# Loading the second unit's rows and gates in the tile program, right behind the plan of units

## The chip, the cores and the metric

One Trainium2 chip, one core of it. The metric is the device time of one launch in microseconds (us). The five engines are PE (TensorE), ACT (ScalarE), DVE (VectorE), POOL (GpSimd) and SP (SyncE, which here only issues transfers). PEld is TensorE's weight load, and a name with q (SPq, DVEq) is the engine's own sequencer at a register, wait, branch or DMA-issuing instruction.

## What is computed

Pooled attention, then a mixture of experts on its output, all in fp32:

```
k_p, v_p = mean of k, v over groups of 8 along the sequence (576 -> 72)
attn     = softmax(q @ k_p.T / 8) @ v_p          # 8 batches x 8 heads, head size 64
x        = attn as [4608, 512]
e        = argmax(x @ w_gate)                    # one of 8 experts for each row
out[row] = gate[row] * (relu(x[row] @ w1[e]) @ w2[e])   # 512 -> 1024 -> 512
```

## The kernel before

**Two programs in one launch.** The first is a tile program (`attention`, then `plan`): waits between its instructions are put in for it from the tiles and DRAM tensors that they read and write, and the order on each engine is the order in which the code is written. It runs the attention in 36 tiles of 128 rows, picks each row's expert, and scatters the row with its gate and its token number to the DRAM tensor `dispatched` (`xs` in the code), where every expert has a region. `plan` (lines 651 to 707, on VectorE) then cuts the regions into units of at most 512 rows and writes the table `tab`, one line for each unit: how many halves of 128 rows it has (column K_U), where its four blocks of 128 rows begin (K_ROW), whether the expert changes. Lines 704 to 706 write the last columns.

The second is the expert program (`experts`, from line 710): five programs written out by hand, one for each engine, with semaphores of its own. It stands in one critical section of the tile program. SP enters that section for all (line 727): it waits there for what is outstanding, and the other engines wait for SP (under line 1521).

**A unit in the expert program.** SP loads the unit's rows (`xload`, line 1225): four blocks of 256 KB into the buffer XE[u % 2], line 1249, and four gates of 1 KB (gate and token of 128 rows) into GT, line 1238. PE transposes the rows (`xt`, line 806, matmuls on line 812), ACT and DVE write them as a high and a low part (lines 1030 and 1045), PE multiplies by w1 (`mm1`, line 859, eight pieces f of 24 matmuls), ACT and DVE form the hidden layer (lines 967 and 988), PE multiplies by w2 (line 881), DVE scales by the gate (line 1170), POOL scatters to the output (line 1349).

**Around the change.** Unit 0 (the first 512 rows of expert 0) is begun in the tile program already: its rows and gates are loaded at lines 435 and 436, its transposes stand at line 452, and six of its eight pieces of the first product run on line 462 under and behind `plan`. `last_hidden` (line 643) is the last of that. SP's last work in the tile program are two transfers of empty rows behind the regions of experts 0 and 1 (line 636, with their places from line 635).

In the expert program PE runs the last two pieces of unit 0's first product (line 859), then transposes blocks 0 and 1 of unit 1 (`xt01(1)`), multiplies the first 12 matmuls of unit 0's last block by w2, transposes blocks 2 and 3 of unit 1 (`xt23(1)`) and goes on with w2. The third group of transposes waits until DVE has written the low part of block 0, the fourth until it has written that of block 1. SP marks unit 0's loads as landed (lines 1313 to 1316), issues `xload(1)` with line numbers read from `tab` by value loads (line 740), and then the eight weight loads of expert 1 (line 1321). POOL's six transfers of empty rows behind the other regions (line 1344) wait for unit 1's loads; SP's `xload(2)` waits for those six.

Of the kernel before, what the change touches and what calls it, by code (L numbers as in the profile page):

```python
# [10 lines left out]
F32 = mybir.dt.float32  # L11
# [7 lines left out]
P = 128  # L19
B, H, S, D = 8, 8, 576, 64  # L20
N, DM, NE, FF = 4608, 512, 8, 1024
# [14 lines left out]
CAP = N + P  # L36
# [11 lines left out]
K_U, K_SW, K_ROW, K_ST, K_AH, NK = 0, 1, 2, 6, 7, 8  # L48
# [30 lines left out]
def attention(ctx, outer, tc, q, k, v, wg, w1v, w2v, xs, W, cst, carry, tab, banks):  # L79
    nc = tc.nc  # L80
# [5 lines left out]
    early, u0 = ExitStack(), {"XE": cst["keep"].tile([P, 4, DM], F32, name="XE0"), "GT": cst["keep"].tile([P, NU, 4, 2], F32, name="GT")}  # L86
# [356 lines left out]
    def x_open():  # L443
        early.close()
        m1 = outer.enter_context(tc.tile_pool(name="m1", bufs=1, side="right", reuse_waits="tile"))
        u0["H"] = m1.tile([P, 2, 8, 512], F32R, name="H")
        u0["X"] = m1.tile([P, 2, 4, 512], F32R, name="X")

    def x_split(s):
        bank, o = (pm, pq)[s % 2], slice(s * P, (s + 1) * P)  # L450
# [194 lines left out]
            hidden(f)  # L645
            multiply(12)

    return u0, more_hidden, last_hidden


def plan(tc, sb, carry, cst, tab, between, after):
# [59 lines left out]
def experts(ctx, tc, xs, w1v, w2v, out, tab, W, ident, empty, scr, u0, banks):  # L711
    nc = tc.nc
    sb = ctx.enter_context(tc.tile_pool(name="m2", bufs=1))
    ST = sb.tile([P, 8, 1024], F32, name="ST")
    XE, GT = (u0["XE"], sb.tile([P, 4, DM], F32, name="XE1")), u0["GT"]
    X, H = u0["X"], u0["H"]
    XH, XL, HH, HL = X[:, 0], X[:, 1], H[:, 0], H[:, 1]
    Y2 = sb.tile([64, 512], F32, name="Y2")
# [6 lines left out]
    pe, act, dve, sp, pool = nc.tensor, nc.scalar, nc.vector, nc.sync, nc.gpsimd  # L725

    with tc.tile_critical():
        names = ("P_xt", "P_h", "P_y", "A_x", "A_h", "A_s1", "A_s2", "V_x", "V_h", "V_y", "V_s1", "V_s2", "V_1", "G_y", "G_s1", "G_s2")
        Q = {n: tc.alloc_semaphore(n) for n in names}
        sx = [[tc.alloc_semaphore(f"sx{i}{s}") for s in range(4)] for i in range(2)]  # L730
        st = [tc.alloc_semaphore(f"st{i}") for i in range(2)]
# [6 lines left out]
        def entry(eng, a, u, lo, hi):  # L738
            r = regs.get((eng, a, u))
            return eng.value_load(tab[u : u + 1, a : a + 1], min_val=lo, max_val=hi) if r is None else r  # L740
# [389 lines left out]
        def ahead(eng, yes, no):  # L1130

            with eng.If(u0[eng] == 1):
                yes()
            with eng.Else():
                no()
# [19 lines left out]
        def dve_unit(u):  # L1155
# [45 lines left out]

            dve.wait_ge(st[u % 2], 64 * (u // 2 + 1))
            dve.reciprocal(out=GT[:, u, :, 0], in_=GT[:, u, :, 0])
            n = entry(dve, K_U, u, 1, 8)
            if u > 0:
                hidden_lo(u)
# [18 lines left out]
        def xload(u):  # L1225


            if u == 2:
                sp.wait_ge(se, 16 * (NE - 2))
            if u >= 2:  # L1230
                sp.wait_ge(Q["P_xt"], 4 * (u - 1))

            rows_of = []

            def gates():

                for s in range(4):
                    sp.dma_start(out=GT[:, u, s, :], in_=xs[ds(rows_of[s], P), DM:]).then_inc(st[u % 2], 16)

            def block(s, apart, rows=True):  # L1240
                r = rows_of[s]
                to, sem = XE[u % 2][:, s, :], sx[u % 2][s]
                if rows and apart:
                    for j in range(4):
                        o = slice(32 * j, 32 * j + 32)
                        sp.dma_start(out=to[o].rearrange("p (g d) -> p g d", g=4),
                                     in_=xs[ds(r, P), j * P : (j + 1) * P].rearrange("(g t) d -> t g d", g=4)).then_inc(sem, 16)
                elif rows:
                    sp.dma_start(out=to, in_=xs[ds(r, P), 0:DM]).then_inc(sem, 16)
                    sp.sem_inc(sem, 48)  # L1250
                else:
                    sp.sem_inc(sem, 64)

            rows_of.extend(entry(sp, K_ROW + s, u, 0, NE * CAP - P) for s in range(4))
            n = entry(sp, K_U, u, 1, 8)

            def blocks(apart):
                for s in range(2):
                    block(s, apart)
                with sp.If(n > 4):  # L1260
                    block(2, apart)
                    with sp.If(n > 6):
                        block(3, apart)
                    with sp.Else():
                        block(3, apart, False)
                with sp.Else():
                    for s in range(2, 4):
                        block(s, apart, False)

            if u < 2:  # L1270
                blocks(False)
                return gates()
            with sp.If(entry(sp, K_U, u - 1, 1, 8) > 2):
                blocks(True)
            with sp.Else():
                blocks(False)
            gates()
# [33 lines left out]
        def sp_start():  # L1311
            def yes():
                sp.sem_inc(Q["P_h"], AF_PE)
                sp.sem_inc(Q["P_xt"], 4)
                for s in (*sx[0], st[0]):
                    sp.sem_inc(s, 64)

            ahead(sp, yes, lambda: xload(0))
            xload(1)
            for i in range(8):  # L1320
                sp.dma_start(out=ST[:, i, :].rearrange("p (c f) -> p c f", c=4 if i < 4 else 2), in_=load_piece(w1v, w2v, 1, i)).then_inc(sg[i], 16)
            count(sp)
# [202 lines left out]
```

## Time and profile before

| what | us |
|---|---|
| median of 3 runs | 635.15 (633.09 to 635.31) |
| the profiled execution | 631.38 |
| its span, first to last instruction | 629.6 |
| TensorE busy | 602.3 (96%) |
| VectorE / ScalarE / GpSimd busy | 354.4 / 240.2 / 240.7 |

The profiled execution is 3.77 us under the median, and 1.78 us of it lie outside the span. All times of rows are microseconds from the start of the span; durations are microseconds or, where a row gives min/median/max, nanoseconds. In a row of the timeline the last bracket is the idle time of that engine ahead of the instruction and what ended it.

### The profile page before, as it was taken

What the parts mean: (1) busy time and instruction counts of PE and PEld (TensorE: products, weight loads), DVE (VectorE), ACT (ScalarE), POOL (GpSimd) and SP (SyncE); (2) the same over time, 40 slices, a digit from 0 to 9 for tenths busy, and PEclk for the clock granted to TensorE, in tenths of its full rate; (3) what the DMA queues carried; (4) which work ended last, traced back from release to release, by engine and by line L of the source; (5) the groups of instructions that cost most, each with busy time, mean ns of one, the idle gap of its engine ahead of it and who ended that gap; (6) DMA issues with size and microseconds to landing.
All of it is one profiled execution on the core that took longest, in us unless ns stands there. A gap on an engine that the chain in (4) does not pass through costs nothing.

```text
span 629.6 us, 13468 instructions
## 1 busy us (share of the span) xinstructions
PE 602.3 (96%) x4412; PEld 513.0 (81%) x4412; DVE 354.4 (56%) x731; ACT 240.2 (38%) x453; POOL 240.7 (38%) x289
## 2 busy tenths in 40 slices
PE   6989999999997999999999999999998999999995
PEld 6778978888876888889898889888897888888994
DVE  7698887889762124467777433854156664133220
ACT  2577666886512014065354311523034641011110
POOL 7457656744421121468445311251107660101101
PEclk9999999999999999999999999999999899999999
DMA  9999996992324930619667551075105453100001
GB/s 326 363 267 258 300 311 209 254 265 70 125 111 135 300 107 2 216 41 297 221 173 267 153 170 36 3 210 167 40 33 164 132 147 71 55 0 36 36 4 53
DMA packets 93937, 96.47 MB, mean 153 GB/s; under 512 B 43102, under 2 KB 74846, under 8 KB 93792
## 3 DMA queue, kind: packets, MB, share of 16 engines
q1 hardware_dynamic: 85808, 74.27, 41.0%
q0 software_dynamic: 7440, 20.50, 8.8%
q8 instruction: 60, 0.98, 0.6%
q14 instruction: 85, 0.70, 0.4%
q10 hardware_dynamic: 544, 0.02, 0.0%
HBM read 72.68 MB, written 26.00 MB: 157 GB/s over the span
## 4 chain that ended last, share of the span: by engine, by line
PE 76%; DVE 6%; issue 5%; DMA 3%; POOL 3%; ACT 3%; SPq 2%; DVEq 0%; ACTq 0%; POOLq 0%
PE pU L881 33%; PE pP L859 20%; PE pq L859 10%; PE pU L299 4%; DMA XE<-in_v_dram 2%; PE pP L283 2%; PE pP L462 2%; POOL dispatched L406 2%; PE pS L263 2%; PE pq L253 1%; SPq L228 1%; ACT W L1057 1%; PE pm L207 1%; DVE mx L267 1%; PE pq L462 1%
## 5 line engine op out<-in xcount | busy, mean ns | idle before, releaser
L881 PE MATMUL pU<-W,H 128*128 128x512 f32 x912 | 216.2, 397 | 0.0
L881 PEld LDWEIGHTS pU<-W,H 128*128 128x128 f32 x912 | 171.3, 188 | 41.0
L859 PE MATMUL pP<-X,W 128*128 128x512 f32 (+3 forms) x748 | 144.0, 347 | 3.7 <-DVEq L1398 1.5
L859 PEld LDWEIGHTS pP<-X,W 128*128 128x128 f32 x748 | 123.6, 189 | 20.4 <-DVEq L1398 2.0
L1349 POOL DMA_INDIRECT out_dram<-Y,GT x51 | 53.0, 1039 | 193.3 <-DVE Y L1170 167.4
L1065 POOL TENSOR_TENSOR W<-ST,W 128x1024 fp32r<-128x1024 f32 x30 | 77.4, 2591 | 89.9 <-ACT W L1057 89.4
L967 ACT ACTIVATE H<-pP 128x512 fp32r<-128x512 f32 (+1 forms) x67 | 35.9, 536 | 196.7 <-PE pP L859 158.1
L1170 DVE TENSOR_SCALAR Y<-pU,GT 128x512 f32<-128x512 f32 x36 | 26.9, 749 | 110.5 <-PE pU L881 109.0
L988 DVE SCALAR_TENSOR_TENSOR H<-pP,H 128x512 fp32r<-128x512 f32 (+2 forms) x73 | 42.1, 579 | 71.5 <-ACT H L967 69.0
L859 PE MATMUL pq<-X,W 128*128 128x512 f32 (+3 forms) x364 | 73.7, 351 | 1.1 <-DVE H L988 0.6
L859 PEld LDWEIGHTS pq<-X,W 128*128 128x128 f32 x364 | 60.8, 191 | 10.1 <-DVE H L988 1.1
L1057 ACT CAST W<-ST 128x1024 fp32r<-128x1024 f32 x56 | 57.1, 1054 | 2.9 <-DMA ST<-in_moe_w_dram 2.9
L299 PE MATMUL pU<-V,pt 110*128 110x146 f32 (+3 forms) x468 | 56.7, 283 | 1.4 <-ACT pt L284 0.8
L299 PEld LDWEIGHTS pU<-V,pt 110*128 110x128 f32 (+3 forms) x468 | 51.4, 179 | 3.1 <-ACT pt L284 1.8
L1065 DVE TENSOR_TENSOR W<-ST,W 128x1024 fp32r<-128x1024 f32 x26 | 46.8, 1801 | 3.5 <-ACT W L1057 2.5
L967 ACT ACTIVATE H<-pq 128x512 fp32r<-128x512 f32 (+1 forms) x33 | 17.8, 541 | 79.5 <-PE pq L859 55.1
L406 POOL DMA_INDIRECT dispatched<-xe,ix x36 | 38.0, 1054 | 15.6 <-POOL ix L368 7.0
L988 DVE SCALAR_TENSOR_TENSOR H<-pq,H 128x512 fp32r<-128x512 f32 (+2 forms) x35 | 20.8, 595 | 28.2 <-ACT H L967 20.3
L284 ACT COPY pt<-pP 110x384 f32<-110x384 f32 x72 | 30.8, 479 | 6.1 <-PE pP L283 4.9
L276 ACT ACTIVATE P<-sd 128x576 f32<-128x576 f32 x36 | 24.8, 689 | 19.3 <-DVE sd L270 16.2
L172 POOL TENSOR_TENSOR raw<-raw 128x768 f32<-128x768 f32 (+1 forms) x18 | 27.0, 1498 | 12.1 <-DMA raw<-in_v_dram 11.4
L267 DVE TENSOR_REDUCE mx<-pS 128x8 f32<-128x576 f32 x36 | 27.1, 752 | 6.8 <-PE pS L263 4.4
(186 smaller groups left out, 621.8 us busy)
## 6 DMA issues: line engine op xcount, KB each, us to landing
ST<-in_moe_w_dram SPq DMA_DIRECT2D x56, 512.0 KB, 4.6
raw<-in_k_dram SPq DMA_DIRECT2D x12, 768.0 KB
raw<-in_v_dram SPq DMA_DIRECT2D x11, 768.0 KB
XE<-dispatched SPq DMA_DIRECT2D x104, 64.0 KB, 2.0
qa<-in_q_dram SPq DMA_DIRECT2D x24, 256.0 KB
w<-in_moe_w_dram SPq DMA_DIRECT2D x8, 512.0 KB
XE<-dispatched SPq DMA_DIRECT2D x15, 256.0 KB, 3.8
qa<-in_q_dram SPq DMA_DIRECT2D x2, 1024.0 KB
```

Of the source, the lines that this page charges most:

```text
L172: return lambda: eng.tensor_tensor(out=out, in0=raw[:, :, 0:n], in1=raw[:, :, n : 2 * n], op=ALU.add)
L267: nc.vector.tensor_reduce(out=mx, in_=s4, axis=AX.X, op=ALU.max)
L284: take(out=pt[t][a][0:R], in_=pPs[a][0:R, 0 : 3 * P])
L299: nc.tensor.matmul(pu[p0 : p0 + n, a, h * VW : (h + m) * VW], lhsT=pt[t][a][0:r, c % 3 * P + p0 : c % 3 * P + p0 + n], rhs=Vs[g % 2][0:r, ...
L406: apart(nc.gpsimd.indirect_dma_start(out=xs, out_offset=bass.IndirectOffsetOnAxis(ap=at, axis=0), in_=rows, in_offset=None))
L859: r = pe.matmul(out=pH[g % 3][:, :m], lhsT=w1s(w, f, k), rhs=x, start=i == 0, stop=i == len(passes) - 1)
L881: r = pe.matmul(out=pY[:, s % 2, :], lhsT=h, rhs=w[:, k * 512 : (k + 1) * 512], start=start and i == 0, stop=stop and i == len(ps) - 1, sk ...
L967: act.activation(out=HH[:, f, o], in_=src[:, o], func=AF.Relu).then_inc(Q["A_h"], 1)
L988: return dve.scalar_tensor_tensor(out=dst[:, f, to], in0=src[:, at], scalar=0.0, in1=f32(HH[:, f, at]), op0=ALU.max, op1=ALU.subtract)
L1057: act.copy(out=(W1H if i < 4 else W2H)[:, o], in_=ST[:, i, :]).then_inc(Q["A_s1" if i < 4 else "A_s2"], 1)
L1065: eng.tensor_tensor(out=(W1L if i < 4 else W2L)[:, o], in0=ST[:, i, :], in1=f32((W1H if i < 4 else W2H)[:, o]), op=ALU.subtract).then_inc( ...
L1349: pool.indirect_dma_start(out=out, out_offset=bass.IndirectOffsetOnAxis(ap=GT[:, u, s, 1:2].bitcast(I32), axis=0), in_=Y[:, s, :], in_offs ...
```

## The change

The buffer XE1, which holds the rows of odd units, moves from the expert program's pool to the pool that the attention opens for unit 0 (`x_open`). A new function `second_load` reads the four places of unit 1's blocks from the second line of `tab` and issues unit 1's four blocks and four gates on SP; it is called behind `plan`, ahead of `last_hidden`. In the expert program SP's `xload(1)` goes, and SP marks those loads as landed at once. All four blocks are loaded whatever the unit's size; the old code left out blocks that the unit does not have. Two smaller edits: DVE drains behind the reciprocal of a unit's gates (line 1203, 13 times in this execution), and from unit 2 on SP waits ahead of a unit's gates until DVE has written the first hidden piece of the unit two before.

```diff
--- before.py
+++ after.py
@@ -445,6 +445,7 @@
         m1 = outer.enter_context(tc.tile_pool(name="m1", bufs=1, side="right", reuse_waits="tile"))
         u0["H"] = m1.tile([P, 2, 8, 512], F32R, name="H")
         u0["X"] = m1.tile([P, 2, 4, 512], F32R, name="X")
+        u0["XE1"] = m1.tile([P, 4, DM], F32, name="XE1")
 
     def x_split(s):
         bank, o = (pm, pq)[s % 2], slice(s * P, (s + 1) * P)
@@ -645,7 +646,20 @@
             hidden(f)
             multiply(12)
 
-    return u0, more_hidden, last_hidden
+    def second_load():
+        rows = [nc.sync.value_load(tab[1:2, K_ROW + s : K_ROW + s + 1], min_val=0, max_val=NE * CAP - P) for s in range(2)]
+        for s in range(4):
+            if s == 2:
+                rows += [nc.sync.value_load(tab[1:2, K_ROW + s : K_ROW + s + 1], min_val=0, max_val=NE * CAP - P) for s in range(2, 4)]
+            nc.sync.dma_start(out=u0["XE1"][:, s, :], in_=xs[ds(rows[s], P), 0:DM])
+        for s in range(4):
+            nc.sync.dma_start(out=u0["GT"][:, 1, s, :], in_=xs[ds(rows[s], P), DM:])
+
+    def at_last():
+        second_load()
+        last_hidden()
+
+    return u0, more_hidden, at_last
 
 
 def plan(tc, sb, carry, cst, tab, between, after):
@@ -712,7 +726,7 @@
     nc = tc.nc
     sb = ctx.enter_context(tc.tile_pool(name="m2", bufs=1))
     ST = sb.tile([P, 8, 1024], F32, name="ST")
-    XE, GT = (u0["XE"], sb.tile([P, 4, DM], F32, name="XE1")), u0["GT"]
+    XE, GT = (u0["XE"], u0["XE1"]), u0["GT"]
     X, H = u0["X"], u0["H"]
     XH, XL, HH, HL = X[:, 0], X[:, 1], H[:, 0], H[:, 1]
     Y2 = sb.tile([64, 512], F32, name="Y2")
@@ -1201,6 +1215,7 @@
 
             dve.wait_ge(st[u % 2], 64 * (u // 2 + 1))
             dve.reciprocal(out=GT[:, u, :, 0], in_=GT[:, u, :, 0])
+            dve.drain()
             n = entry(dve, K_U, u, 1, 8)
             if u > 0:
                 hidden_lo(u)
@@ -1234,6 +1249,8 @@
 
             def gates():
 
+                if u >= 2:
+                    sp.wait_ge(Q["V_h"], 8 * (u - 2) + 1)
                 for s in range(4):
                     sp.dma_start(out=GT[:, u, s, :], in_=xs[ds(rows_of[s], P), DM:]).then_inc(st[u % 2], 16)
 
@@ -1267,7 +1284,7 @@
                     for s in range(2, 4):
                         block(s, apart, False)
 
-            if u < 2:
+            if u == 0:
                 blocks(False)
                 return gates()
             with sp.If(entry(sp, K_U, u - 1, 1, 8) > 2):
@@ -1316,7 +1333,8 @@
                     sp.sem_inc(s, 64)
 
             ahead(sp, yes, lambda: xload(0))
-            xload(1)
+            for s in (*sx[1], st[1]):
+                sp.sem_inc(s, 64)
             for i in range(8):
                 sp.dma_start(out=ST[:, i, :].rearrange("p (c f) -> p c f", c=4 if i < 4 else 2), in_=load_piece(w1v, w2v, 1, i)).then_inc(sg[i], 16)
             count(sp)
```

## Rows read from the trace of the kernel before

**Rows 1.** The page's first two parts: busy time of PE with its share of the span, and in 40 equal slices the tenths of full speed that TensorE's clock was granted.

```profile
PE 602.3 (96%) x4412; PEld 513.0 (81%) x4412; DVE 354.4 (56%) x731; ACT 240.2 (38%) x453; POOL 240.7 (38%) x289
...
PEclk9999999999999999999999999999999899999999
```

**Rows 2.** The view of waits for PE from 200 us to the end, its first line: who waited for whom, us in total, times, the longest.

```profile
PE pP L859 <- DVE H L988: 1.4, 2, 1.1
```

**Rows 3.** The timeline of PE from 184 to 206 us: start, length, line, tiles, count, idle time before and what ended it.

```profile
186.22 2.96 PE L462 MATMUL pq<-X,W 128*128 128x512 f32 x12
190.71 5.88 PE L859 MATMUL pP<-X,W 128*128 128x512 f32 x24 [1.53 <-DVEq L1398]
197.46 0.75 PE L812 MATMUL pS<-ident,XE 128*128 128x128 f32 x4 [0.86 <-DMA XE<-dispatched]
199.48 0.75 PE L812 MATMUL pS<-ident,XE 128*128 128x128 f32 x4 [1.28 <-DMA XE<-dispatched]
199.98 3.05 PE L881 MATMUL pU<-W,H 128*128 128x512 f32 x12
202.87 1.11 PE L812 MATMUL pS<-ident,XE 128*128 128x128 f32 x8
203.74 2.59 PE L881 MATMUL pU<-W,H 128*128 128x512 f32 x10
```

**Rows 4.** The view of waits of SP's own queue, whole span.

```profile
SPq L435 <- DMA dispatched<-xe,ix: 19.3, 3, 12.6
...
SPq L727 <- PE pq L462: 4.2, 1, 4.2
...
SPq L727 <- DMA dispatched<-empty: 3.5, 2, 2.8
```

**Rows 5.** The last instruction of line 727 on SP between 180 and 190 us, behind which the other engines are let in: count, ns min/median/max, first and last start in us.

```profile
L727 SPq NOP  x1: 18/18/18, 189.3 to 189.3; - x1
```

**Rows 6.** The timeline of all engines around the end of the plan: the last write of the table, and SP's two transfers of empty rows.

```profile
178.61 1.49 SPq L636 DMA_DIRECT2D dispatched<-empty  x2
...
181.82 0.22 DVE L706 TENSOR_SCALAR tab<-off,R 128x4 int32<-128x4 f32 x1
```

**Rows 7.** Two stretches of the view by stretches, behind those two transfers and up to PE's last tile-program matmul: length, busy time of PE, PEld, DVE, ACT, POOL, granted clock, share of the DMA engines, GB/s.

```profile
182.05:183.70 1.65, 1.65 (x9) 1.33 (x8) 0.58 (x1) 0.08 (x1) 0.00 (x0) 1.00 0.04 6
183.70:189.20 5.50, 5.48 (x24) 4.09 (x22) 0.69 (x1) 0.52 (x1) 0.00 (x0) 1.00 0.00 0
```

**Rows 8.** The chain that ended last, in order of time, where it runs over SP: one value load (three pieces, the next begins at 192.00), and the first two blocks of unit 1.

```profile
191.39 0.28 SPq L740
...
192.00 0.26 SPq L740
...
194.36 0.37 SPq L1249
...
194.99 4.45 DMA XE<-dispatched
```

**Rows 9.** The instructions of line 1238 on SP between 190 and 203 us, and those of line 1343 on POOL, which come right behind POOL's wait for unit 1's gates.

```profile
L1238 SPq DMA_DIRECT2D GT<-dispatched x4: 333/333/1089, 197.1 to 199.4; - x4
...
L1343 POOLq TENSOR_LOAD <-tab x6: 288/296/318, 202.2 to 208.1; - x6
```

**Rows 10.** The page's list of DMA issues: count, KB each, median us from issue to landing.

```profile
XE<-dispatched SPq DMA_DIRECT2D x104, 64.0 KB, 2.0
```

**Rows 11.** The timelines of SP and POOL around unit 0's loads in the tile program: the last gate, and the next scatter to the same tensor, which waits for it.

```profile
158.12 0.43 SPq L436 DMA_DIRECT2D GT<-dispatched  x1
...
163.72 1.02 POOL L406 DMA_INDIRECT dispatched<-xe,ix  x1 [5.85 <-DMA GT<-dispatched]
```

**Rows 12.** The timeline of DVE from 197 to 202 us.

```profile
199.35 0.18 DVE L1203 RECIPROCAL GT<-GT 128x4 f32<-128x4 f32 x1 [1.34 <-issue]
199.47 0.69 DVE L1045 TENSOR_TENSOR X<-pS,X 128x512 fp32r<-128x512 f32 x1
200.88 0.69 DVE L1045 TENSOR_TENSOR X<-pS,X 128x512 fp32r<-128x512 f32 x1 [0.72 <-ACT X L1030]
```

**Rows 13.** The view by stretches again (columns as in group 7): the pause between the programs, a stretch with little work for PE, and the one stretch of the expert program in which the granted clock was half.

```profile
189.18:190.71 1.53, 0.00 (x1) 0.00 (x0) 0.00 (x0) 0.00 (x0) 0.00 (x0) 1.00 0.00 0
...
484.58:487.52 2.94, 1.22 (x8) 1.00 (x8) 2.29 (x6) 1.33 (x3) 2.17 (x3) 1.00 0.88 295
...
488.12:491.53 3.41, 3.41 (x19) 3.41 (x18) 1.11 (x4) 2.29 (x4) 3.05 (x3) 0.50 0.87 270
```

**Rows 14.** The chain that ended last at a small unit's end: a drain that is there already, and the one reciprocal of gates on the chain behind 200 us.

```profile
286.19 0.03 DVEq L1165
286.22 0.05 issue
...
288.47 0.16 DVE GT L1203
```

**Rows 15.** Timelines of DVE, ACT and SP: the first hidden piece of unit 1, the first use of expert 1's weights, and the rows of units 2 and 3.

```profile
223.00 5.35 SPq L1246 DMA_DIRECT2D XE<-dispatched  x8
...
227.15 0.69 DVE L988 SCALAR_TENSOR_TENSOR H<-pq,H 128x512 fp32r<-128x512 f32 x1 [2.57 <-issue]
...
247.54 2.02 ACT L1057 CAST W<-ST 128x1024 fp32r<-128x1024 f32 x2
...
263.04 1.65 SPq L1249 DMA_DIRECT2D XE<-dispatched  x3
```

## The prediction, made before the changed kernel was run

> **What bounds the kernel now.** I read the page first: PE is busy for 602.3 of the 629.6 us of the span [rows 1], so a change can give or take only what PE stands still for, or the clock it runs at. The waits of PE say where it stands still: behind 200 us the largest entry is 1.4 us over two waits [rows 2], so nothing that the change touches late in the run has much to give. The place of the change is the passage from the tile program to the expert program, and there the timeline of PE shows three holes [rows 3]. PE's last tile-program matmuls end at 186.22 + 2.96 = 189.18. Then 1.53 us pass until line 859 begins at 190.71; that is the entry of the critical section. After those 24 matmuls PE waits 0.86 us for block 0 of unit 1 and, four transposes later, 1.28 us for block 1. These last two, 2.14 us together, are what the change aims at.
>
> What opens the entry is in SP's own waits [rows 4]: line 727 waited 3.5 us for the two transfers of empty rows to land, and last, for 4.2 us, for PE's matmuls. So the entry asks for every transfer that is under way as well as for the engines, and only because the transfers were long done did PE end it; SP passed it at 189.3 [rows 5], 0.1 us behind PE. The same list shows that a tile-program load from `dispatched` waits for the writes to it to land (line 435, 12.6 us at the longest).
>
> **The change part by part.**
>
> *Removed: PE's waits for unit 1's rows.* First the bound from PE alone. Eight transposes without a wait take 203.74 - 202.87 = 0.87 us until w2 begins [rows 3]. Behind line 859, which ends at 196.59, w2 would then begin near 197.3 instead of 199.98, 2.7 us earlier. But DVE is next. The fourth group of transposes waits for the low part of block 1, and DVE cannot begin block 0's before its reciprocal at 199.35, ahead of which it was reading its registers and waited for nobody [rows 12]. With the transposes early, the two low parts follow one another: 199.47 + 0.1 for the new drain + 2 x 0.69 = 200.95. PE arrives there at 197.3 + 2.8 for 12 matmuls = 200.1 and waits some 0.9 us; four transposes of 0.12 later w2 goes on at 201.45 instead of 203.74. **Gain 2.3 us**, between 2.1 (the two waits alone) and 2.7.
>
> *Added: eight transfers that the entry has to wait for.* The table is complete at 181.82 + 0.22 = 182.04 [rows 6]. Two value loads at 0.6 us (192.00 - 191.39) [rows 8] end at 183.2, hidden behind the empty rows: their transfers begin at 178.61 and 180.1 [rows 6], SP's 3.5 us of waiting for them from 180.1 on end at 183.7 [rows 4], and the DMA engines fall to a share of 0.04 behind 182.05 and to 0.00 behind 183.70 [rows 7]. Block 0 can so be issued at 183.9. Block 1 follows 0.63 us later (194.99 - 194.36) [rows 8], and is done issuing at 185.15; the two other value loads take it to 186.35, blocks 2 and 3 to 187.6. The four gates began between 197.1 and 199.4, where the first took 1.09 us and the others 0.33 [rows 9], so a pace of 0.53 to 0.77: the last gate is issued at 189.2 to 189.9. Its landing is not shown by itself. From below, the page has 2.0 us for the landing of 64 KB [rows 10]; POOL, which waited for these very loads, read its table at 202.2, 2.8 us behind the last issue [rows 9]; and the last gate of unit 0 was issued at 158.12 while the scatter that waited for it began at 163.72, 5.6 us later [rows 11]. I take 2.2, since the DMA engines are idle in this stretch [rows 7], as they were not beside unit 0. So the last gate lands at 191.4 and SP passes the entry at some 191.6 instead of 189.3. **Cost 2.3 us.** The ends: issues at 0.43 us each [rows 11] and a landing of 2.0 give 183.7 + 1.2 + 7 x 0.43 + 2.0 = 189.9, a delay of 0.7; the slow issue and 5.6 give 195.5, a delay of 6.2.
>
> *What the longer pause does to TensorE's clock.* PE has no work between 189.18 and the entry, so its pause grows from 1.53 to 3.8 us. After 1.53 us the granted clock stayed at 1.00, which is 2.4 GHz [rows 13]. After a stretch of 2.94 us in which PE was busy for 1.22, it was 0.50 (1.2 GHz) from 488.12 for 3.41 us [rows 13]. A pause of 3.8 us without any matmul is more idleness than either row has, and the second is the nearer. In 3.41 us at half speed PE does half its work: **cost 1.7 us**; the ends are 0 and twice that. The Trainium skill (TensorE: Matmul & The Clock Gate, Part 1: The HAM clock gate) makes the slow clock the default that only activity lifts. By that rule the fall is due, and the sum is 1.8; by the row of the 1.53 us pause alone it would be 0.1.
>
> *Moved earlier, at no cost.* Without `xload(1)` SP comes to the weights of expert 1 some 6 us earlier and POOL to its six transfers some 7 us earlier. Both go on overlapping each other; ACT first casts those weights at 247.54 [rows 15], and the rows of unit 2, which wait for POOL's six, were issued at 223.00 and are wanted late in unit 1. There is nothing behind them that PE waits for. XE1 in its new place lies over buffers whose readers were through long before 183 us. If that cover failed, one more wait of the size of 1.3 us would stand at the passage.
>
> *The drains.* The present drain of line 1165 holds DVE for 0.03 us and 0.05 of idling [rows 14]. The chain shows one reciprocal of gates on it behind 200 us, at 288.47 [rows 14]. **Cost 0.1 us**; if all 13 were on it, 1.1.
>
> *The wait ahead of the gates.* SP's loads of unit 3 were issued from 263.04 on, while the first hidden piece of unit 1, for which they will wait, was being written at 227.15 [rows 15]. Behind SP's wait stand only the stagings of the next weights, which wait for later steps of the same units. Cost nothing; with the cover gone, a gate would be late at line 1170, and the bound is one landing of 2 us.
>
> **The sum.** -2.3 + 2.3 + 1.7 + 0.1 = +1.8 us. The profiled execution would go from 631.38 to 633.2. It lies 3.77 us under the median of the runs shown, so I put the difference on the median: 635.15 + 1.8 = 636.95, said as 637.0. A measurement of this kernel can tell about 0.5% from no change, 3.2 us; the forecast is no change that can be told.
>
> **The rivals.**
>
> *The clock holds* (0.18). The loads land as forecast, PE's pause falls so that the clock stays at 2.4 GHz as it did after 1.53 us. Sum +0.1: 635.3. Against it speaks the row at 488.12.
>
> *Slower: the last gate lands late* (0.17). Unit 0's gates took up to 5.6 us to their reader. With that in place of 2.2 the entry is opened 3.4 us later still: 635.15 + 1.8 + 3.4 = 640.4, and the longer pause makes the clock's fall surer. It decides from the point where the entry is more than 3.7 us late (3.7 - 2.3 + 1.7 + 0.1 = 3.2), a last gate landing behind 192.9. For it: eight issues and four value loads in one queue, the gates at its end. Against it: nothing else moves at that time.
>
> *The loads are free* (0.07). The entry does not wait for them, or they land before PE's last matmul. Then only the gain and the drain are left: 635.15 - 2.2 = 632.95, still within 0.5%. The Trainium skill (DMA: Bandwidth & Descriptors, Rules for kernel authors) advises just this, to issue early, compute, and wait late. Against it: line 727 did wait for transfers [rows 4], and 189.9 is the earliest landing that the rows allow.
>
> *Not what it says, or something elsewhere* (0.06). The loads are held behind a wait that the tile program adds and I do not see, or the stretch of half clock at 488.12 comes or goes with the new phase: 1.7 us either way around 635.3, with a tail to both sides.
>
> **How the numbers follow.** The forecast has 0.52. Its own bounds (landing 2.0 to 2.8, gain 2.1 to 2.7, clock 0 to 3.4) make about 634.5 to 639. The range takes in the clock rival and the lower half of the late gate, and at the bottom almost the free loads: 633.0 to 640.0. Left out are the later half of the late gate (0.09), most of the free loads (0.05) and tails (0.04). Slower by over 0.5%, that is above 638.3: 0.17, nearly all from the late gate and the upper end of the clock. Faster by over 0.5%, under 631.97: 0.04, from the tails alone, for even free loads do not reach it. Within: 0.79.
>
> **What the changed profile would show.** Right: line 812's waits for XE gone from PE's list; in SP's waits line 727 last released by transfers from `dispatched`, not by PE; a pause of PE of 3 to 5 us ahead of line 859, and behind it a stretch of granted clock 0.50; w2's second stretch no earlier than now; POOL's transfers of line 1344 some 5 us earlier. Wrong: line 859 beginning near 190.7 would mean that the entry does not wait, or that the loads are faster than every row here; a pause of 3.8 us with the clock at 1.00 would take the clock term out; a gain at the passage that is lost again behind 250 us would mean that I overlooked a late consumer.

## The result: slower by 0.5 to 0.75%, and the profile after

| | before | after | ratio, 95% interval |
|---|---|---|---|
| first measurement, medians of 6 runs each | 635.09 us | 639.83 us | 1.0075 [1.0054, 1.0096] |
| second, on another chip, medians of 35 and 12 runs | 635.68 us | 638.54 us | 1.0048 [1.0029, 1.0067] |
| profiled execution | 631.38 us, span 629.6 | 638.89 us, span 637.2 | |

The change costs 4.7 us by the first measurement and 2.9 by the second. The forecast was +1.8: the sign holds, the range (633.0 to 640.0) holds by 0.2 us, the size does not. Chips differ by some 5 us on the kernel before (medians of 634.65, 630.98 and 635.68 on the three of the experiments), so everything below goes by ratios against before on the same chip.

The page after, its first two parts, as in [rows 1]:

```profile
PE 604.9 (95%) x4412; PEld 515.3 (81%) x4412; DVE 355.3 (56%) x731; ACT 240.3 (38%) x453; POOL 241.4 (38%) x289
...
PEclk9999999999998899999999999999999899999999
```

PE is busy 2.6 us longer with the same 4412 matmuls, and the clock has two new dips near 200 us. So a part of the loss is clock and the rest is waiting. The timeline of PE at the passage, columns as in [rows 3]:

```profile
187.70 2.96 PE L463 MATMUL pq<-X,W 128*128 128x512 f32 x12
194.04 7.41 PE L873 MATMUL pP<-X,W 128*128 128x512 f32 x24 [3.38 <-DVEq L1416]
201.29 1.11 PE L826 MATMUL pS<-ident,XE 128*128 128x128 f32 x8
202.16 3.05 PE L895 MATMUL pU<-W,H 128*128 128x512 f32 x12
206.88 1.33 PE L826 MATMUL pS<-ident,XE 128*128 128x128 f32 x8 [1.67 <-DVE X L1059]
```

Read it against [rows 3] from the end of the tile program, which the profiled execution reaches at 190.66 instead of 189.18: 1.48 us were lost before that, the distance hardly changes from 56 us on, and the change touches nothing there. The pause grew from 1.53 to 3.38 us (+1.85). The 24 matmuls take 7.41 instead of 5.88 us (+1.53). The two waits for `XE` are gone: eight transposes in one row. But a new wait of 1.67 us for DVE stands at the third group, so that from the end of the 24 matmuls to that group 5.43 us pass instead of 6.28. Of the gain of 2.3 only 0.85 arrived.

The stretches of the clock, columns as in [rows 7]; the third is the time in which ACT and DVE read their registers:

```profile
194.40:197.81 3.41, 3.41 (x10) 2.64 (x9) 1.29 (x2) 1.08 (x2) 2.68 (x3) 0.50 0.36 96
...
208.05:211.46 3.41, 3.41 (x10) 2.69 (x9) 1.36 (x3) 0.85 (x3) 0.00 (x0) 0.50 1.01 277
...
201.50:205.00 3.50, 3.50 (x20) 2.82 (x18) 0.75 (x2) 0.59 (x1) 1.27 (x3) 1.00 1.03 372
```

Two stretches of 3.41 us at a granted clock of 0.50 (1.2 GHz): the first behind the pause of 3.38, the second behind the new wait of 1.67. At half speed the second costs 3.41 / 2 = 1.7.

SP's waits, and line 741's last instruction (the old 727), as in [rows 4, 5]:

```profile
SPq L741 <- DMA GT<-dispatched: 1.2, 2, 1.0
```

```profile
L741 SPq NOP  x2: 13/16/18, 192.6 to 636.0; - x2
```

The first of these two stands at the entry, which is now opened by the gates' landing: SP passes it at 192.6, 1.9 us behind PE's end. The chain that ended last, in order of time, says how SP came there:

```profile
181.57 3.81 DMA dispatched<-empty
185.52 0.37 SPq L654
...
186.50 0.27 SPq L653
...
188.88 0.33 SPq L656
...
190.46 1.71 DMA GT<-dispatched
```

The empty rows have landed at 185.38, the blocks go out from 185.52 with the value loads of line 653 between them, the last gate at 190.46, and it lands 1.71 us later.

What came earlier, by the timelines of SP and POOL (start, length, line, tiles, count):

```profile
195.07 9.26 SPq L1339 DMA_DIRECT2D ST<-in_moe_w_dram  x8
...
196.38 0.60 POOL L1362 DMA_DIRECT2D dispatched<-empty  x1 [0.17 <-issue]
```

Before, they began at 199.81 (6.71 us for the eight) and 203.53. They now run beside the value loads with which ACT and DVE read unit 1's sizes. Those, after (count, ns min/median/max, first and last start):

```profile
L754 ACTq TENSOR_LOAD <-tab x2: 984/1006/1029, 202.6 to 203.8; - x2
L794 ACTq TENSOR_LOAD <-tab x1: 813/813/813, 201.5 to 201.5; - x1
L754 DVEq TENSOR_LOAD <-tab x2: 449/763/1077, 203.5 to 204.9; - x2
L794 DVEq TENSOR_LOAD <-tab x1: 881/881/881, 202.3 to 202.3; - x1
```

and the same before:

```profile
L740 ACTq TENSOR_LOAD <-tab x2: 274/276/277, 197.2 to 197.7; - x2
L780 ACTq TENSOR_LOAD <-tab x1: 277/277/277, 196.6 to 196.6; - x1
L740 DVEq TENSOR_LOAD <-tab x2: 306/306/306, 198.1 to 198.7; - x2
L780 DVEq TENSOR_LOAD <-tab x1: 317/317/317, 197.5 to 197.5; - x1
```

Three reads on ACT took 0.83 us and now 2.8; three on DVE 0.93 and now 2.4. Ahead of its reciprocal, and of the low part that PE waits for, DVE now idles 2.82 us, where it was 1.34 [rows 12].

Last, the small units. PE, after, with the holes of interest in brackets:

```profile
279.46 1.22 PE L873 MATMUL pq<-X,W 128*128 128x256 f32 x8 [1.22 <-DVE H L1002]
...
296.24 3.97 PE L873 MATMUL pP<-X,W 128*128 128x384 f32 x21 [1.13 <-issue]
```

Before, they were 0.61 and 0.30; the distance between the kernels grows by 0.68 and 0.45 there. The ledger of the profiled executions is thus 1.85 + 1.53 - 0.85 + 1.7 + 1.1 = 5.3 us for the change, plus 1.5 from ahead of the passage, against 7.5 between their times; 0.7 I did not place. Against the medians' 4.7 and 2.9, the ledger without the second stretch of half clock is 3.6.

The profiles are one execution each, but the mean granted clock is on record for every execution: 0.9916 on average over the 12 of the second measurement, 0.9940 over the 35 of before beside them. An estimate from these is that the clock took (0.9940 - 0.9916) x 637 = 1.5 of the 2.9 us, if PE had work throughout, and waiting the other 1.4.

### The profile page after: what moved, and what is told of

Read it like the earlier page. It is cut to its first block, busy times and chain, and to the rows that moved or that the text cites. A ratio compares the mean times of both kernels' runs of the same rounds, so it can differ in the third digit from the quotient of the medians.

```text
span 637.2 us, 13480 instructions
## 1 busy us (share of the span) xinstructions
PE 604.9 (95%) x4412; PEld 515.3 (81%) x4412; DVE 355.3 (56%) x731; ACT 240.3 (38%) x453; POOL 241.4 (38%) x289
## 4 chain that ended last, share of the span: by engine, by line
PE 71%; DVE 9%; issue 8%; DMA 4%; POOL 3%; ACT 3%; SPq 1%; DVEq 1%; ACTq 0%; POOLq 0%
PE pU L895 30%; PE pP L873 21%; PE pq L873 10%; PE pU L299 3%; DMA XE<-in_v_dram 2%; PE pP L283 1%; DMA raw<-in_v_dram 1%; DVE mx L267 1%; PE pS L263 1%; PE pq L253 1%; DVE xe L315 1%; POOL raw L172 1%; POOL dispatched L406 1%; ACT W L1071 1%; DVE sd L270 1%
## 5 line engine op out<-in xcount | busy, mean ns | idle before, releaser
L873 PE MATMUL pP<-X,W 128*128 128x512 f32 (+3 forms) x748 | 145.6, 349 | 6.6 <-DVEq L1416 3.4
L873 PEld LDWEIGHTS pP<-X,W 128*128 128x128 f32 x748 | 124.9, 191 | 23.5 <-DVEq L1416 3.8
L1002 DVE SCALAR_TENSOR_TENSOR H<-pP,H 128x512 fp32r<-128x512 f32 (+2 forms) x73 | 42.0, 579 | 70.8 <-ACT H L981 69.1
L1002 DVE SCALAR_TENSOR_TENSOR H<-pq,H 128x512 fp32r<-128x512 f32 (+2 forms) x35 | 20.8, 594 | 27.9 <-ACT H L981 24.0
```

Source lines behind the costliest of these rows:

```text
L873: r = pe.matmul(out=pH[g % 3][:, :m], lhsT=w1s(w, f, k), rhs=x, start=i == 0, stop=i == len(passes) - 1)
L1002: return dve.scalar_tensor_tensor(out=dst[:, f, to], in0=src[:, at], scalar=0.0, in1=f32(HH[:, f, at]), op0=ALU.max, op1=ALU.subtract)
```

## The experiments

Three groups, each on one chip with its own runs of before: e1 to e4, e5 to e8, e9 to e12. The theory: the entry waits for the gates, the pause lowers the clock, and the streams moved earlier spoil the gain. The rivals: the drain, the added loads alone, and the issuing pace of SP.

**e1_added: the transfers alone.** Before, with the loads also made in the tile program into tiles that nobody reads; the old `xload(1)` stays.

```diff
+        u0["XE1"] = m1.tile([P, 4, DM], F32, name="XE1")
+        u0["GT1"] = cst["keep"].tile([P, 4, 2], F32, name="GT1")
...
+            nc.sync.dma_start(out=u0["GT1"][:, s, :], in_=xs[ds(rows[s], P), DM:])
...
-    return u0, more_hidden, last_hidden
+    return u0, more_hidden, at_last
```

> The kernel before, with the eight transfers of second_load added in the tile program into buffers that nobody reads; the old loads of unit 1 stay where they were, so nothing is gained and nothing moves earlier. It prices the entry alone. Theory (the entry waits for the last gate, and the longer pause lowers the clock): PE's pause ahead of line 859 is 3.2 to 3.8 us instead of 1.53, behind it 3.4 us at half clock, and the time is 3.4 us (0.5%) over before; PE still waits for XE. Rival (the entry costs little, the loss of the changed kernel is elsewhere, in the drains and in what was moved): under 1 us over before.

Ratio 1.003 [1.0012, 1.0048], +1.9 us, where I had expected 3.4. PE and the stretch of half clock:

```profile
194.71 5.87 PE L874 MATMUL pP<-X,W 128*128 128x512 f32 x24 [3.29 <-DVEq L1413]
201.63 0.75 PE L827 MATMUL pS<-ident,XE 128*128 128x128 f32 x4 [1.05 <-DMA XE<-dispatched]
```

```profile
203.16:206.58 3.42, 2.93 (x9) 2.54 (x10) 1.51 (x3) 0.58 (x1) 0.00 (x0) 0.50 0.60 145
```

The entry term is shown by itself: +1.76 of pause, and slower in time, with nothing moved and nothing gained. The clock fell only 8.4 us behind the pause's end (0.4 in the change), after the waits for `XE`, and the 24 matmuls ran at full speed; why so late stays open.

**e2_warm: work in the pause.** After, with eight more matmuls that nobody reads behind the last hidden piece.

```diff
+        for _ in range(8):
+            nc.tensor.matmul(pm, lhsT=w1s(W[:, 0], 0, 0), rhs=u0["X"][:, 0, 0, :], start=True, stop=True, skip_group_check=True)
```

> The changed kernel, with eight extra matmuls of 128x512 into a bank that nobody reads behind the tile program's last ones; PE so works until about the landing of the last gate and the pause in which it has nothing to do is some 1.5 us again. Theory (clock): the first half-clock stretch goes and line 859 (now 873) takes 5.9 us instead of 7.4; the time falls by 1.5 us against the changed kernel, to about 1.005 of before; if the fall at 208 us came from the first fall, that goes too, and it is 3 us. Rival (the pause costs by its length alone): no change against the changed kernel, 1.0075, or more by what the extra matmuls add.

Ratio 1.0107 [1.0085, 1.0128]. PE:

```profile
195.09 7.42 PE L875 MATMUL pP<-X,W 128*128 128x512 f32 x24 [2.29 <-DVEq L1418]
207.00 1.95 PE L828 MATMUL pS<-ident,XE 128*128 128x128 f32 x8 [4.49 <-issue]
```

The expectation failed: 2.29 us of pause were left and the clock fell all the same. The 4.49 us of waiting for nothing that the profile shows make the time unfit to judge the clock. One packet of instructions (0.02 MB) was moved between 203 and 206 us; whether PE waited for it is not shown. Inconclusive.

**e3_late_both: the two streams held back.** After, with SP's weights and POOL's six transfers of empty rows waiting until DVE has written unit 1's first two low parts.

```diff
+            sp.wait_ge(Q["V_x"], 6)
             for i in range(8):
                 sp.dma_start(out=ST[:, i, :]...
...
+            pool.wait_ge(Q["V_x"], 6)
             for e in range(2, NE):
```

> The changed kernel, with SP's eight weight loads of expert 1 and POOL's six transfers of empty rows held until DVE has written the low part of block 1 of unit 1 (V_x at 6); these are the two streams that the change moved earlier. Theory (DVE's and ACT's value loads took 0.45 to 1.08 us instead of 0.31 and 0.28 because these streams ran beside them): value loads at 0.28 to 0.31 again, PE's wait ahead of the third group of transposes 0.9 us instead of 1.67 or less, no second half-clock stretch; the time falls by 1 us from the wait alone and by 2.5 us with the clock, to about 1.004 of before. Rival (the value loads are slow for another reason, such as code being loaded at that time): value loads stay at about 1 us and the time at 1.0075.

Ratio 1.0031 [1.0011, 1.0052]. PE, and the value loads:

```profile
195.06 7.43 PE L873 MATMUL pP<-X,W 128*128 128x512 f32 x24 [3.39 <-DVEq L1418]
...
206.43 1.31 PE L826 MATMUL pS<-ident,XE 128*128 128x128 f32 x8 [0.18 <-DVE X L1059]
```

```profile
L754 ACTq TENSOR_LOAD <-tab x2: 277/278/280, 203.1 to 203.6; - x2
L754 DVEq TENSOR_LOAD <-tab x2: 304/304/305, 204.0 to 204.6; - x2
```

The reads are back at 0.28 and 0.30 us, PE's wait at 0.18. From the end of the 24 matmuls (202.49) to the third group 3.94 us pass, 6.28 - 3.94 = 2.34 less than before: the forecast's gain, at its size. Pause and half clock stay, and no second stretch of half clock follows. The time by itself does not tell e3 from the change (1.0048 [1.0029, 1.0067] in e9); the trace does, and so do e11 and e12 below.

**e4_nodrain: the drain.** After without it.

```diff
             dve.reciprocal(out=GT[:, u, :, 0], in_=GT[:, u, :, 0])
-            dve.drain()
```

> The changed kernel without the drain behind the reciprocal of the gates. Theory (a drain holds DVE's sequencer, which then passes its branches and register reads only behind the reciprocal, at each small unit): the first reduction of the small unit near 275 us begins 0.3 us behind the reciprocal instead of 0.96, the waits of PE at 278 and 295 us fall from 1.2 and 1.1 to about 0.6 and 0.4 us, and the time falls by 1 to 1.5 us, to about 1.0055 of before. Rival (a drain costs 0.1 us, and the later holes come from the shifted clock): the time stays within 0.3 us.

Ratio 1.0038 [1.0016, 1.0061]. The two holes at the small units are back at 0.60 and 0.45 us, the passage is as in after (pause 3.09, wait 1.73). So the drain makes the holes and not the passage. No second stretch of half clock follows the wait of 1.73, so such a wait does not by itself bring one. The twelve times spread from 633.76 to 641.89 us, and the ratio cannot be told from that of the change.

**e5_late_weights and e6_late_pool: one stream held.** The edit of e3, its first line alone and its second alone.

```diff
+            sp.wait_ge(Q["V_x"], 6)
             for i in range(8):
```

```diff
+            pool.wait_ge(Q["V_x"], 6)
             for e in range(2, NE):
```

> The changed kernel with only SP's eight weight loads held until DVE has written the low part of block 1 of unit 1; POOL's six transfers stay early. Theory (the weights, 4 MB written into SBUF, slow the value loads): value loads of ACT and DVE near 202 us at 0.28 and 0.31 us, the wait of PE there under 0.3 us, the time as with both held, about 1.003 of before. Rival (POOL's transfers slow them): value loads near 0.8 to 1.1 us and the wait 1.7 us, the time at 1.0075.

> The changed kernel with only POOL's six transfers of empty rows held until DVE has written the low part of block 1 of unit 1; the weight loads stay early. Theory (the weights slow the value loads): value loads near 0.8 to 1.1 us and a wait of PE of about 1.7 us as in the changed kernel, the time near 1.0075. Rival (POOL's transfers): value loads at 0.28 and 0.31 us, the wait under 0.3 us, about 1.003.

Ratios 1.0006 [0.9987, 1.0024] and 1.0011 [0.9997, 1.0025]. I had taken the weights alone to be the culprit, or else POOL's six alone. Neither is: each edit by itself brings the wait down, to 0.39 and 0.18 us. But the two are not alike. Three of e5's reads still take 0.52 to 0.56 us, none of e6's does. The reads of e5, then one row of e6 (the rows with x3 and x4 hold later reads too):

```profile
L794 ACTq TENSOR_LOAD <-tab x1: 532/532/532, 198.5 to 198.5; - x1
L754 ACTq TENSOR_LOAD <-tab x4: 275/280/555, 199.2 to 204.8; - x4
L754 DVEq TENSOR_LOAD <-tab x3: 303/306/519, 199.9 to 206.9; - x3
```

```profile
L754 ACTq TENSOR_LOAD <-tab x4: 274/280/289, 199.6 to 205.2; - x4
```

How full the transfer engines are at the reads, by the same view by stretches as above, e5 first, then e6:

```profile
198.50:201.30 2.80, 2.80 (x17) 2.40 (x16) 0.75 (x2) 1.18 (x3) 1.27 (x3) 1.00 0.56 213
```

```profile
199.10:201.50 2.40, 2.40 (x16) 2.08 (x15) 0.75 (x2) 1.30 (x3) 0.00 (x0) 1.00 0.87 263
```

The share of the DMA engines is 0.56 and 0.87 here, 0.85 before, and 1.03 in after. In the five profiles with both streams at the reads (after, e2, e4, e9, e11) it is 1.03 to 1.06, and the reads take 0.35 to 1.16 us. In the eight without POOL's stream at the reads it is 0.00 to 0.93, and they take 0.27 to 0.32. So it is not the fullness alone: with POOL's stream alone three of six reads are slow at 0.56, and without it none is at 0.93 (e1).

**e7_nodrain_late: everything avoidable taken out.** The edits of e3 and e4 together.

```diff
-            dve.drain()
...
+            sp.wait_ge(Q["V_x"], 6)
...
+            pool.wait_ge(Q["V_x"], 6)
```

> The changed kernel without the drain and with both streams held; what is left of the change is the earlier load and the later entry. If the two prices add (2.8 us from holding, 2.4 us from the drain, of 4.7), the time is within 1 us of before, ratio 0.998 to 1.001: the pause (+1.8) and the half clock behind it (+1.5) against the waits saved (-2.7 or so). Rival (the two overlap, one hiding the other): ratio 1.002 to 1.004.

Ratio 0.9997 [0.9974, 1.0020]. Pause 3.12, 24 matmuls 7.42, then 3.71 us to the third group, 2.57 less than before. Gain and entry pay for each other: within the interval, what the change aimed at is worth what its own entry costs.

**e8_early_issue: the aim without the entry.** Before, with unit 1's blocks 0 and 1 each issued right behind the read of its own row, instead of behind all the value loads.

```diff
+            if u == 1:
+                for s in range(2):
+                    rows_of.append(entry(sp, K_ROW + s, u, 0, NE * CAP - P))
+                    block(s, False)
+                rows_of.extend(entry(sp, K_ROW + s, u, 0, NE * CAP - P) for s in range(2, 4))
...
-                for s in range(2):
+                for s in range(2 if u != 1 else 0):
                     block(s, apart)
```

> The kernel before, where SP in its xload(1) reads the place of block 0, issues block 0, reads the place of block 1, issues block 1, and only then reads the other two places and the count; the entry is untouched. Theory (PE waited for SP's five value loads of 0.56 us, not for the transfers as such): block 0 is issued 2.3 us and block 1 1.8 us earlier, PE's waits for XE fall from 2.14 to under 0.5 us, the second stretch of w2 begins 1.7 us earlier, the time is 0.997 of before. Rival (the transfers, not the issue, set the landing, or DVE's registers do): ratio 0.999 to 1.001.

Ratio 0.9961 [0.9942, 0.998], 628.08 against 630.98 us: faster than both kernels. PE:

```profile
190.60 5.86 PE L859 MATMUL pP<-X,W 128*128 128x512 f32 x24 [1.53 <-DVEq L1404]
196.30 1.12 PE L812 MATMUL pS<-ident,XE 128*128 128x128 f32 x8
...
200.18 1.32 PE L812 MATMUL pS<-ident,XE 128*128 128x128 f32 x8
```

and SP, where the four blocks are one row of the timeline:

```profile
192.04 4.97 SPq L1249 DMA_DIRECT2D XE<-dispatched  x4
```

The blocks go out from 192.04 instead of 194.36 [rows 8], PE's waits for `XE` are gone, the pause is 1.53 as before, and the clock does not fall at the passage. To the third group 3.72 us pass, 2.56 less; the ratio gives (1 - 0.9961) x 631 = 2.5. That the two agree is in part luck: the executions of e8 also had a higher granted clock than those of before beside them (medians 0.9965 and 0.994), by an estimate from these up to 0.0025 x 629 = 1.6 us. How much of the 2.5 is the waits and how much the clock elsewhere in the run, these runs do not separate.

**e9_after_again: the change once more.** No edit.

> The changed kernel once more, unaltered, so that it stands beside the three runs below on one chip. Theory: 1.0075 of before again (interval 1.0054 to 1.0096 the first time), a pause near 3.4 us, value loads of ACT and DVE at 0.8 to 1.1 us near 202 us. Rival (a part of the first loss belonged to that chip or that hour): under 1.004.

Ratio 1.0048 [1.0029, 1.0067]. Pause 3.44, 24 matmuls 7.42, wait 1.29, reads 0.43 to 0.88 us: the same picture, but no second stretch of half clock behind the wait (an earlier one stands at 170.64, ahead of the passage). That stretch, 1.7 us of the first ledger, is not in every execution.

**e10_drain_alone: before with the drain.** The one line of e4, added to before.

```diff
             dve.reciprocal(out=GT[:, u, :, 0], in_=GT[:, u, :, 0])
+            dve.drain()
```

> The kernel before with nothing but the drain behind the reciprocal of the gates. Theory (DVE's sequencer stands at the drain until the pipe is empty, and then has branches and register reads ahead of it that it used to pass meanwhile; PE feels it at the small units): the hole of PE near 272 us grows from 0.6 to 1.2 us, one near 289 us to about 1.1 us, and the time rises by 1.0 to 1.5 us, ratio 1.002. Rival (a drain costs 0.1 us as the prediction had it): ratio 1.000 and the holes as before.

Ratio 0.9994 [0.9976, 1.0012]: no price that can be measured, where I had expected 1.0 to 1.5 us. Yet the trace of PE has holes like those of after:

```profile
276.60 1.22 PE L859 MATMUL pq<-X,W 128*128 128x256 f32 x8 [1.23 <-DVE H L988]
...
293.40 4.50 PE L859 MATMUL pP<-X,W 128*128 128x384 f32 x24 [0.77 <-issue]
```

1.23 and 0.77 for 0.61 and 0.30. The interval (-1.5 to +0.8 us) leaves room for most of these 1.1, and the matter stays open between 0 and 0.8.

**e11_static: no value loads in the tile program.** After, with fixed rows as addresses of the loads (512 to 1023, which is where unit 1's blocks lie for these inputs).

```diff
-            nc.sync.dma_start(out=u0["XE1"][:, s, :], in_=xs[ds(rows[s], P), 0:DM])
+            nc.sync.dma_start(out=u0["XE1"][:, s, :], in_=xs[512 + s * P : 640 + s * P, 0:DM])
...
-            nc.sync.dma_start(out=u0["GT"][:, 1, s, :], in_=xs[ds(rows[s], P), DM:])
+            nc.sync.dma_start(out=u0["GT"][:, 1, s, :], in_=xs[512 + s * P : 640 + s * P, DM:])
```

> The changed kernel with the places of unit 1's blocks written as constants (rows 512 to 1023, which is where they are for these inputs; the four value loads of the table in the tile program are left out), so the eight transfers are issued right behind the empty rows. Theory (the entry is late by what SP does between the plan and the last gate): the last gate lands near 189.5 us, the pause is 1.5 to 2.0 us, no half clock follows it at once, and the time is 3 us under the changed kernel, ratio 1.002 to 1.003, the rest being the drain and the slow value loads. Rival (the entry waits for something else): the pause stays over 3 us and the ratio at 1.0075.

Ratio 1.0046 [1.0025, 1.0066]. PE:

```profile
199.38 7.42 PE L870 MATMUL pP<-X,W 128*128 128x512 f32 x24 [3.49 <-DVEq L1413]
```

The expectation, a pause of 1.5 to 2.0 us, failed: 3.49. SP's pace does not set the entry.

**e12_static_nodrain_late: the same with e7's edits.** e11, without the drain and with both streams held.

```diff
-            dve.drain()
...
+            sp.wait_ge(Q["V_x"], 6)
...
+            pool.wait_ge(Q["V_x"], 6)
```

> The same constants, without the drain, and with the weight loads and POOL's six transfers held until DVE has written the low part of block 1 of unit 1: all three costs taken out, only the early load left. Theory (the change's gain of 2.3 us is real and was paid away by the pause with its clock, the drain and the slow value loads): PE has no wait for XE, a pause of 1.5 to 2.0 us, ratio 0.996 to 0.997. Rival (something else of the change, the place of XE1 in memory for one, costs as well): ratio 0.999 or more.

Ratio 1.0009 [0.9993, 1.0025], where I had expected 0.996 to 0.997. SP's timeline, and the stretches from the first block's issue to the last gate's landing and of half clock:

```profile
185.44 1.77 SPq L651 DMA_DIRECT2D XE<-dispatched  x4
187.25 1.85 SPq L653 DMA_DIRECT2D GT<-dispatched  x4
```

```profile
185.40:191.80 6.40, 5.26 (x23) 3.90 (x21) 0.69 (x1) 0.29 (x1) 0.00 (x0) 1.00 0.57 165
...
192.65:199.47 6.82, 5.82 (x14) 4.56 (x15) 1.29 (x2) 1.38 (x3) 1.80 (x1) 0.50 0.03 6
```

SP issued all eight in 3.7 us instead of after's 5.3, but the last gate landed 3.1 us behind its issue instead of 1.7, so that from the first issue to the last landing 6.3 us pass in e12 and 6.7 in after. In e11 it is 6.5. Issuing faster does not shorten it; what does set it is not shown, for the transfer engines were at a share of 0.57 in the first stretch. The first block waits for the last write to `dispatched` (3.6 us in this profile's list of SP's waits). The half clock held twice as long as at the other passages, and the 24 matmuls took 8.51 us. With the pause that is 1.47 + 2.63 = 4.1 us lost against 2.56 gained, so the rival's other cost, such as the place of XE1 in memory, is not needed for this profile; no run tested it by itself. Against e11, on the same chip, e12 is 2.3 us faster, and the intervals only touch: holding the streams and leaving out the drain show in the time, and e10 gives the drain alone no price.

The passage in all profiles; the fourth column is the time from the end of the 24 matmuls to the third group of transposes, which holds the gain (6.28 before), the fifth the half clock at the passage:

| kernel | pause, us | 24 matmuls, us | to the third group, us | half clock from, us | ratio |
|---|---|---|---|---|---|
| before | 1.53 | 5.88 | 6.28 | none | 1 |
| e8 | 1.53 | 5.86 | 3.72 | none | 0.9961 |
| e10 | 1.53 | 5.87 | 6.74 | none | 0.9994 |
| after | 3.38 | 7.41 | 5.43 | 194.40, 208.05 | 1.0075 |
| e9 | 3.44 | 7.42 | 5.05 | 197.95 | 1.0048 |
| e11 | 3.49 | 7.42 | 5.03 | 200.71 | 1.0046 |
| e4 | 3.09 | 7.23 | 5.49 | 193.24 | 1.0038 |
| e2 | 2.29 | 7.42 | 9.51 | 196.13, 206.37 | 1.0107 |
| e3 | 3.39 | 7.43 | 3.94 | 195.17 | 1.0031 |
| e5 | 4.01 | 7.41 | 4.16 | 190.99 | 1.0006 |
| e6 | 4.27 | 7.28 | 3.95 | 191.46 | 1.0011 |
| e7 | 3.12 | 7.42 | 3.71 | 192.29 | 0.9997 |
| e12 | 3.00 | 8.51 | 3.72 | 192.65 | 1.0009 |
| e1 | 3.29 | 5.87 | 7.72 | 203.16 | 1.0030 |

In e10 the time to the third group holds one wait of 2.68 us for `XE`, in place of the two of [rows 3]. The columns add up to more than the ratio for e5 and e6: there PE came to the passage at 187.0 and 187.5, some 2 us ahead of before and e8 (189.2, 189.1), and the entry opened at 191.0 and 191.8, hardly later than before's 190.7. A pause is a loss only as far as the work ahead of it did not end early, and one profile a kernel cannot say how often it does.

Half clock also stands where the change touches nothing (the end of the span left out): for 3.41 us near 490 us in before [rows 13], after and e10 and in no other profile; at 170 us in e9 and, for 10.24 us, in e11; in the first 60 us in e6, e7 and e8. Each stretch of 3.41 can cost 1.7 us, so the whole time of one profiled execution says little to within 2 us.

## Why the prediction was right in sign and too low

The forecast was no change that can be told, with 0.79 for less than 0.5% either way. Both intervals lie above 1. The first measurement, 0.75%, is in the part that had 0.17; the second, 0.48%, is just inside the 0.5%.

**Gain 2.3: right, but not delivered.** e3 shows 2.34, e8 2.56, each with the reads at their old length. In the change it is 0.85, and 1.23 in the repetition. Counted to w2's second stretch, as the prediction did, all are some 0.2 lower, for the fourth group then waits a little: 2.13 in e3 (5.02 us for 7.15), 2.33 in e8 (4.82), 0.63 in the change (6.52).

**"Moved earlier, at no cost": the step that failed.** I looked at the moved transfers' own overlap and at what waits for them, and found nobody. I did not look at what reads beside them. With both streams beside them (share 1.03) the reads of registers on ACT and DVE take 1.5 to 3.7 times as long, and PE waits 1.67 us for DVE. The step even named this price ("one more wait of the size of 1.3 us") and gave it no chance. By e3's 2.34 against after's 0.85 it was 1.5 us in the gain, and in one of two profiles of the change another 1.7 from a second stretch of half clock. With 1.5 the sum of +1.8 would have been +3.3, between the two measurements. That holding either stream takes away most of the wait is shown. What in the streams slows the reads is open: full engines fit thirteen of the fourteen profiles, and e5 speaks against them as the only cause.

**Entry 2.3: right in mechanism, sized 0.4 too high, and built from the wrong pace.** The gates' landing opens the entry (1.2 us of SP's waiting), and the pause grew by 1.85; the landing, 2.2 in the sum, took 1.71. The working built the rest from eight issues and four value loads in SP's queue. e11 and e12 take the value loads out, the eight are issued 1.6 us faster, the gates land about as much later behind their issue, and the pause stays. What sets the 6.3 to 6.7 us of these 1 MB is not shown.

**Clock 1.7: right, 1.53 in the change**, and 2.6 at most (e12). All ten kernels with a pause of 2.29 us or more had a stretch of 0.50 at it, nine beginning between 1.0 us before its end (e12) and 1.3 us behind it (e11), and e1 8.4 us behind it; the three with 1.53 had none there. The Trainium skill (TensorE: Matmul & The Clock Gate, Part 1: The HAM clock gate), by which idleness brings the slow clock back, lets one expect a fall at a pause, and these ten agree. That the pause is what does it was not shown by a run that filled it, since e2 failed to.

**Drains 0.1: open.** The trace has 1.1 us at two small units that the chain of before, with one reciprocal on it, did not announce; e10's time does not have them.

**The wait ahead of the gates: nothing, as forecast.** In the change's list of SP's waits it stands with 0.2 us in all (SPq L1255 <- DVE H L1002: 0.2, 1, 0.2); no run leaves it out.

**The rivals.** The clock did not hold, and the loads were not free. The late gate did not come: 1.71 us to its landing, not 5.6. The outcome above 638.3 came, in the first measurement, by a mechanism that was not among the rivals, so its 0.17 did not stand for what happened. The last rival named the stretch near 488 us that comes or goes: it stayed in the profile of the change and is gone in that of its repetition, a swing of 1.7 us that no term has. The advice that stood beside the free loads (the Trainium skill, DMA: Bandwidth & Descriptors, Rules for kernel authors: issue early, wait late) needs its second half: here the entry waits for every transfer at once, and e1, which issues early and waits there, is 1.9 us slower.

## What to carry to other kernels

A load moved ahead of a point that waits for all transfers is paid for there, with the clock's fall on top; here the chance was in the order of issue behind that point, where e8 took the waits away by issuing each block right behind the read of its own address. When a step leaves a queue, ask what that queue does next, and beside what: not only who waits for the transfers that come earlier, but who reads registers while they run. And name a chance for every cover that is assumed to hold.

## What the runs showed of the hardware

- A read of a register from the table took 0.27 to 0.32 us in the eight profiles without POOL's transfers of empty rows beside it (share of the transfer engines 0.00 to 0.93). With those alone (e5, 0.56) three of six took 0.52 to 0.56, and with SP's weights as well (1.03 to 1.06) all took 0.35 to 1.16.
- Four gates of 1 KB behind four blocks of 256 KB landed 1.7 us behind the last issue when issued over 5.3 us (after), and 3.1 and 3.3 us when issued over 3.7 (e12, e11).
- The stretches of half clock lasted 3.41 us in nearly all profiles, 6.82 in e12, although PE was busy for 5.82 of these, and 10.24 in e11 from 169.99 on, with PE busy throughout.
